# A layer norm, windowed attention and gated feed-forward kernel: from three phases with pooled order to one written-out pipeline over 512-token chunks

## The chip, the cores and the metric

The kernel runs on one core of a Trainium2 chip. The metric is device time in microseconds (us). Engine names: PE is TensorE's matmuls and PEld its weight loads, DVE is VectorE, ACT is ScalarE, POOL is GpSimd, and SP is SyncE, which here issues every DMA.

## What is computed

The input `x` has 2048 tokens of 512 features in bf16. Cut to what matters, the reference is:

```python
xn = _layernorm(x)                                   # no gain, no bias
# attention: H = 32 heads of Dh = 16, W = 8 taps, each 2 tokens apart, looking back
q, k, v = split(xn @ wqkv)                           # wqkv is 512 x 1536
logits = einsum("bhsd,bhswd->bhsw", q, k[s - 2*w]) * Dh ** -0.5   # masked where s - 2*w < 0
o = einsum("bhsw,bhswd->bhsd", softmax(logits), v[s - 2*w])
s = o @ wo                                           # wo is 512 x 512
# feed-forward: w_gate, w_up are 512 x 1792, w_down is 1792 x 512
y = (gelu_tanh(xn @ w_gate) * (xn @ w_up)) @ w_down
out = x + s * silu(y)
```

So each token has 8 logits in each of 32 heads, and each logit is a sum over 16 features.

## The kernel before

Weights stay in SBUF. The text of the kernel has phases over all 2048 tokens, and the tile framework's scheduler orders each engine's instructions by priority and readiness, so that pieces of the feed-forward land between the attention's.

1. **Layer norm** (L142 to L165): 16 tiles of 128 tokens. `bn_stats` and `bn_aggr` on DVE, the square root on ACT and a reciprocal on DVE for `rstd`, `xn_t` on DVE, four PE transposes into `tr_ps`, and a DVE copy into `xnT`.
2. **`qkv_phase`** (L181 to L204): for each of four 512-token chunks, 12 outputs of 128 features, each four matmuls of 512 columns. ACT copies `q_sb` and `k_sb` out of PSUM; `vst` goes to `vT_dram`.
3. **`attention_phase`** (L215 to L311): all four chunks lie side by side on the 128 partitions (chunk times head). For each of 8 taps and 4 feature groups DVE makes `prodk` (128 x 2048), and four matmuls with an indicator `ind1` of 128 columns, nearly all of them zero, sum the 16 features of each head into one `L_ps` of 128 rows. One Exp over 128 x 4096, a tree of DVE adds, one reciprocal of 128 x 512 and one multiplication make `attn`. For each of 16 features and 8 taps DVE makes `pv` (128 x 512), and PE adds the taps by multiplying with the identity into `oacc_ps`. The result goes through DRAM into `oT_fm`, and 64 matmuls with `wo_sb` give `s_sb`.
4. **`ffn_phase`** (L322 to L367): for each chunk 14 times four matmuls into `g_ps` and four into `u_ps`; ACT copies `u_bf`, squares `g_ps` and takes a tanh; DVE runs three `scalar_tensor_tensor`s, two of which read PSUM (L342, L347, L351). Then four tiles of 14 matmuls into `y_ps`, a tanh on ACT and one more DVE instruction for `g2`.
5. **Output** (L382 to L390): `x` is loaded a second time; DVE makes `bb` and `o_t`; SP stores.

The feed-forward and the attention have three PSUM banks each, and the transposes two.

Of the kernel before, what the change touches and what calls it, by code (L numbers as in the profile page):

```python
# [14 lines left out]
_DEBUG_MODE = 0
_FFN_FIRST = False
_PSUM_SPLIT = True
_H_ON_GPSIMD = False
# [3 lines left out]
def kernel(  # L22
# [10 lines left out]
):  # L33
    nc = tc.nc
    P = 128
    B, S, D = A_x.shape
    DF = B_w_gate.shape[1]
    H = 32
    DH = D // H
    W = 8  # L40
    DIL = 2
    PAD = 16
    assert (W - 1) * DIL <= PAD
    NT = S // P
# [39 lines left out]
    pstr = ctx.enter_context(tc.tile_pool(name="pstr", bufs=2, space=bass.MemoryType.PSUM))

    x_chunks = []
    for xc in range(NXC):
        xt = xpool.tile([P, XC, D], BF16, name="x_chunk")
# [12 lines left out]
    wu_sb = wpool.tile([P, NC, DF], BF16, name="wu_sb")
    nc.sync.dma_start(out=wu_sb[:], in_=B_w_up.rearrange("(k p) n -> p k n", p=P))
# [327 lines left out]
```

## Time and profile before

| what | us |
|---|---|
| median of 3 runs | 322.67 (322.48 to 322.85) |
| span of the profiled execution, first to last instruction | 319.8 |
| median of the runs less that span | 2.87 |
| DVE busy, share of the span | 245.1, 77% |
| ACT busy, share of the span | 165.8, 52% |

The profile gives the profiled execution as its span; what a run holds outside the span is the 2.87 us between the span and the median. Busy times are sums over the span, so they say nothing of which engine is waited for in a stage; the windows and the chain of waits do. A matmul's own duration (about 0.38 us for 512 columns) overlaps the next one, so PE's pace is read from a stretch and its count.

### The profile page before, as it was taken

How to read it: one execution, taken by the hardware profiler on the slowest of the kernel's cores; microseconds unless marked ns; L12 is line 12 of the kernel's file. 1: busy time of each engine (PE TensorE's matmuls, PEld its weight loads, DVE VectorE, ACT ScalarE, POOL GpSimd, SP SyncE). 2: the span in 40 equal slices, each digit the busy share in tenths (PEclk: the TensorE clock that was granted, in tenths of full speed). 3: DMA queues.
4: the chain of work that ended last, by engine and by line, in shares of the span. 5: the costliest groups of instructions: out<-in, count | busy, mean ns of one | idle time of the engine just before them, and what ended most of it. 6: DMA issues, size and time to landing. Idle time of an engine off the chain costs nothing.

```text
span 319.8 us, 3547 instructions
## 1 busy us (share of the span) xinstructions
PE 287.3 (90%) x1248; PEld 119.6 (37%) x1248; DVE 245.1 (77%) x460; ACT 165.8 (52%) x281; POOL 1.4 (0%) x10
## 2 busy tenths in 40 slices
PE   0698999999998576999999999999999999999993
PEld 0444444444433222444332343344443334443341
DVE  4867710159999699989999999944389995899954
ACT  1155986642201835622222488827558882588811
POOL 1000000000000000000000000000000000000000
PEclk9999999999999956999999999999999999999998
DMA  7997111110000093000000197102410001200012
GB/s 248 395 371 235 66 35 33 67 66 0 2 0 0 1 214 56 1 0 0 2 0 1 28 198 240 61 0 68 132 53 14 2 0 36 87 10 1 0 35 66
DMA packets 17762, 22.57 MB, mean 71 GB/s; under 512 B 1104, under 2 KB 15696, under 8 KB 17744
## 3 DMA queue, kind: packets, MB, share of 16 engines
q1 hardware_dynamic: 17744, 22.34, 23.3%
q8 instruction: 10, 0.16, 0.2%
q14 instruction: 8, 0.07, 0.1%
HBM read 16.04 MB, written 6.29 MB: 70 GB/s over the span
## 4 chain that ended last, share of the span: by engine, by line
PE 48%; DVE 30%; ACT 17%; issue 2%; DMA 1%; DVEq 0%; ACTq 0%
DVE pv L275 13%; PE qkv_ps L181 13%; PE y_ps L358 13%; PE L_ps L223 7%; ACT zt L345 7%; DVE zt L342 7%; ACT zt L341 7%; PE g_ps L322 5%; PE s_ps L304 4%; PE u_ps L331 4%; DVE prodk L215 3%; DVE stats L142 1%; ACT u_bf L339 1%; PE tr_ps L162 1%; DVE hT L351 1%
## 5 line engine op out<-in xcount | busy, mean ns | idle before, releaser
L322 PE MATMUL g_ps<-xnT,wg_sb 128*128 128x512 bf16 x224 | 61.5, 391 | 8.1 <-ACT u_bf L339 2.8
L331 PE MATMUL u_ps<-xnT,wu_sb 128*128 128x512 bf16 x224 | 60.7, 390 | 6.2 <-ACT u_bf L339 3.9
L215 DVE TENSOR_TENSOR prodk<-q_sb,k_sb 128x2048 bf16<-128x2048 bf16 x32 | 37.5, 1222 | 25.0 <-ACT k_sb L196 21.0
L358 PE MATMUL y_ps<-wd_sb,hT 128*128 128x512 bf16 x224 | 55.3, 379 | 0.6
L181 PE MATMUL qkv_ps<-xnT,wqkv_sb 128*128 128x512 bf16 x192 | 43.7, 387 | 0.0
L275 DVE TENSOR_TENSOR pv<-attn,v_arr 128x512 bf16<-128x512 bf16 x128 | 43.0, 416 | 0.0
L342 DVE SCALAR_TENSOR_TENSOR zt<-zt,g_ps 128x512 bf16<-128x512 bf16 x56 | 38.3, 684 | 5.5 <-ACT zt L341 0.7
L345 ACT ACTIVATE zt<-zt 128x512 bf16<-128x512 bf16 x56 | 35.2, 629 | 12.0 <-DVE zt L342 11.6
L281 PE MATMUL oacc_ps<-pv,ident 128*128 128x512 bf16 x128 | 41.2, 378 | 0.0
L351 DVE SCALAR_TENSOR_TENSOR hT<-zt,gu 128x512 bf16<-128x512 bf16 x56 | 38.4, 686 | 3.5 <-ACT zt L345 2.8
L339 ACT ACTIVATE u_bf<-u_ps 128x512 bf16<-128x512 f32 x56 | 33.2, 593 | 14.1 <-PE u_ps L331 13.6
L341 ACT ACTIVATE zt<-g_ps 128x512 bf16<-128x512 f32 x56 | 33.1, 596 | 13.9 <-PE g_ps L322 7.8
L347 DVE SCALAR_TENSOR_TENSOR gu<-g_ps,u_bf 128x512 bf16<-128x512 f32 x56 | 38.3, 684 | 0.2 <-ACT u_bf L339 0.2
L322 PEld LDWEIGHTS <-wg_sb 128*128 128x128 bf16 x224 | 22.1, 99 | 42.6 <-issue 22.8
L331 PEld LDWEIGHTS <-wu_sb 128*128 128x128 bf16 x224 | 22.2, 100 | 33.2 <-issue 9.3
L223 PE MATMUL L_ps<-prodk,ind 128*128 128x512 bf16 x128 | 32.6, 378 | 1.7 <-DVE prodk L215 0.9
L358 PEld LDWEIGHTS <-hT 128*128 128x128 bf16 x224 | 21.5, 97 | 29.0 <-issue 3.3
L181 PEld LDWEIGHTS <-wqkv_sb 128*128 128x128 bf16 x192 | 18.9, 100 | 21.5 <-issue 0.2
L288 ACT ACTIVATE o_arr<-oacc_ps 128x512 bf16<-128x512 f32 x16 | 9.6, 597 | 33.2 <-PE oacc_ps L281 33.2
L367 DVE SCALAR_TENSOR_TENSOR g<-th,y_ps 128x512 bf16<-128x512 bf16 x16 | 10.9, 686 | 20.3 <-ACT th L366 20.3
L366 ACT ACTIVATE th<-y_ps 128x512 bf16<-128x512 f32 x16 | 9.5, 597 | 31.0 <-PE y_ps L358 30.7
L281 PEld LDWEIGHTS <-ident 128*128 128x128 bf16 x128 | 11.7, 96 | 23.3 <-issue 9.5
(41 smaller groups left out, 153.8 us busy)
## 6 DMA issues: line engine op xcount, KB each, us to landing
x_chunk<-in_A_x_dram SPq DMA_DIRECT2D x4, 512.0 KB, 4.8
x_t<-in_A_x_dram SPq DMA_DIRECT2D x16, 128.0 KB, 2.3
vT_dram<-vst SPq DMA_DIRECT2D x16, 128.0 KB, 1.8
oT_dram<-o_arr SPq DMA_DIRECT2D x4, 512.0 KB, 7.8
oT_fm<-oT_dram SPq DMA_DIRECT2D x4, 512.0 KB, 5.2
out_dram<-o_t SPq DMA_DIRECT2D x16, 128.0 KB, 1.7
wg_sb<-in_B_w_gate_dram SPq DMA_DIRECT2D x1, 1792.0 KB, 14.7
wu_sb<-in_B_w_up_dram SPq DMA_DIRECT2D x1, 1792.0 KB, 9.2
```

The costliest lines, as they stand in the source:

```text
L181: nc.tensor.matmul(ps[:], lhsT=wqkv_sb[:, dk, fo * P : (fo + 1) * P], rhs=xnT[:, dk, jq * TQ : (jq + 1) * TQ], start=(dk == 0), stop=(dk = ...
L215: nc.vector.tensor_tensor(out=prodk[:], in0=q_sb[:, c, :], in1=k_sb[:, c, koff : koff + S], op=ALU.mult,)
L223: nc.tensor.matmul(L_ps[:], lhsT=ind1[:, IND1_OFF - o : IND1_OFF - o + P], rhs=prodk[:, jq * TQ : (jq + 1) * TQ], start=(c == 0 and jq == ...
L275: nc.vector.tensor_tensor(out=pv[:], in0=attn[:, w, :], in1=v_arr[:, d, voff : voff + TQ], op=ALU.mult,)
L281: nc.tensor.matmul(oacc_ps[:], lhsT=ident[:], rhs=pv[:], start=(w == 0), stop=(w == W - 1),)
L322: nc.tensor.matmul(g_ps[:], lhsT=wg_sb[:, dk, fc * P : (fc + 1) * P], rhs=xnT[:, dk, jq * TQ : (jq + 1) * TQ], start=(dk == 0), stop=(dk = ...
L331: nc.tensor.matmul(u_ps[:], lhsT=wu_sb[:, dk, fc * P : (fc + 1) * P], rhs=xnT[:, dk, jq * TQ : (jq + 1) * TQ], start=(dk == 0), stop=(dk = ...
L341: nc.scalar.activation(out=zt[:], in_=g_ps[:], func=AF.Square, scale=sqrt_c2)
L342: nc.vector.scalar_tensor_tensor(out=zt[:], in0=zt[:], scalar=c1, in1=g_ps[:], op0=ALU.add, op1=ALU.mult)
L345: nc.scalar.activation(out=zt[:], in_=zt[:], func=AF.Tanh)
L351: heng.scalar_tensor_tensor(out=hT[:, fc, :], in0=zt[:], scalar=1.0, in1=gu[:], op0=ALU.add, op1=ALU.mult)
L358: nc.tensor.matmul(y_ps[:], lhsT=hT[:, fc, tt * P : (tt + 1) * P], rhs=wd_sb[:, fc, :], start=(fc == 0), stop=(fc == NF - 1),)
```

## The change

The kernel's body is written anew. The scheduler is told to keep the order as written (`manual_schedule`), and the order is one pipeline over four chunks `j` of 512 tokens.

- **Layer norm** runs two chunks ahead, tile by tile. `rstd` is an addition and a power of -0.5 on POOL; the copy out of `tr` is on ACT. `x` stays in SBUF and is loaded once. The loads are cut smaller.
- **Logits**: the 128 partitions of `L_ps` now hold 4 taps times 32 heads of one chunk. DVE makes `pk` for one tap, all four feature groups at once (128 x 2048). The indicator `dsum[:, c, :]` has 32 columns; tap `wl` writes partitions `32*wl` to `32*wl + 31`, and four such matmuls, one for each tap, follow one another in `logits`.
- **Softmax**: Exp per half of the taps, straight from PSUM. `denominators` sums taps on PE (32-column `hsum`, 128 columns streamed), DVE takes one reciprocal of 128 x 128, `spread_reciprocals` lays it out by matmuls, and the division comes after the sum over taps, in the DVE instruction that makes `oT`.
- **Values**: `load_v` reads the chunk's `v` from DRAM four times, shifted by the tap. DVE makes `pv` for four features at once; `av_sum` adds over four taps on the partitions and two halves by 32-column matmuls, and its output has the layout that `wo` needs, so the attention's output no longer goes through DRAM.
- **Activations**: `Gelu_apprx_tanh` and `Silu` on ACT in place of the square, tanh and `scalar_tensor_tensor` chains; one DVE multiplication makes `h`.
- **PSUM**: five banks for projections, `y` and `s`; two for the attention; one for transposes.

The diff, cut to its core (removed lines are those of the kernel above; `project` is the same four-matmul loop as before, on `xnT[j]`):

```diff
+    ctx.enter_context(tc.manual_schedule())
...
+    prod = pool("prod", 8)
+    hp = pool("hp", 16)
...
+    sm = pool("sm", 3)
+    sm2 = pool("sm2", 2)
...
+    mm = pool("mm", 5, space=bass.MemoryType.PSUM)
+    att = pool("att", 2, space=bass.MemoryType.PSUM)
+    trp = pool("trp", 1, space=bass.MemoryType.PSUM)
...
+    for t in range(TPQ):
+        load_x(t)
+    for i in range(3):
+        load_w(wqkv_sb, A_wqkv, i * D, (i + 1) * D)
+    load_x(TPQ, TPQ)
+    for lo, hi in ((0, DF // 2), (DF // 2, DF)):
+        load_w(wg_sb, B_w_gate, lo, hi)
+        load_w(wu_sb, B_w_up, lo, hi)
     nc.sync.dma_start(out=wd_sb[:], in_=B_w_down.rearrange("(k p) n -> p k n", p=P))
+    load_x(2 * TPQ, TPQ)
+    load_x(3 * TPQ, TPQ)
+    for g in range(NC):
+        nc.sync.dma_start(
+            out=wo_sb[:, g, :],
+            in_=bass.AP(tensor=A_wo.tensor, offset=g * 4 * D, ap=[[D, 4], [DH * D, H], [1, D]]),
+        )
...
+    dsum = const.tile([P, NC, H], BF16, name="dsum")
+    nc.gpsimd.memset(dsum[:], 0.0)
+    for c in range(NC):
+        nc.gpsimd.memset(dsum[:, c, 8 * c : 8 * c + 8], 1.0)
+        band(dsum[:, c, 8 * c : 8 * c + 8], 0, 16, 16, 1, 8)
+    hsum = const.tile([P, H], BF16, name="hsum")
...
+    hsum = const.tile([P, H], BF16, name="hsum")
+    for j in range(WL):
+        nc.vector.tensor_copy(
+            out=hsum[H * j : H * (j + 1), :], in_=ident[H * j : H * (j + 1), H * j : H * (j + 1)]
+        )
...
+    def moments(t):
+        nc.vector.bn_stats(out=stats[:, t, :], in_=x_sb[:, t, :])
+        nc.vector.bn_aggr(out=mv[:, t, :], in_=stats[:, t, :])
+        nc.gpsimd.tensor_scalar(
+            out=rstd[:, t, :], in0=mv[:, t, 1:2], scalar1=EPS, scalar2=None, op0=ALU.add
+        )
+        nc.gpsimd.tensor_tensor(out=rstd[:, t, :], in0=rstd[:, t, :], in1=mhalf[:], op=ALU.pow)
+    def normalize(t):
+        xn = sm2.tile([P, D], BF16, name="xn")
+        nc.vector.tensor_scalar(
+            out=xn[:], in0=x_sb[:, t, :], scalar1=mv[:, t, 0:1], scalar2=rstd[:, t, :],
+            op0=ALU.subtract, op1=ALU.mult,
+        )
+        transpose(t, xn)
+    def transpose(t, xn):
+        tr = trp.tile([P, NC * P], BF16, name="tr")
+        for c in range(NC):
+            nc.tensor.transpose(tr[:, c * P : (c + 1) * P], xn[:, c * P : (c + 1) * P], ident[:])
+        j, i = divmod(t, TPQ)
+        if i == 0:
+            xnT[j] = xtp.tile([P, NC, TQ], BF16, name="xnT")
         nc.scalar.activation(
+            out=xnT[j][:, :, i * P : (i + 1) * P],
+            in_=tr[:].rearrange("p (c n) -> p c n", c=NC),
+            func=AF.Copy,
+        )
...
+    def qkv(j, fo):
+        which, c = divmod(fo, NC)
+        if fo == 0:
+            st[j]["q"] = qp.tile([P, NC, TQ], BF16, name="q_sb")
+        ps = mm.tile([P, TQ], F32, name="qkv_ps", tag="mm")
+        project(ps, wqkv_sb, fo * P, j)
+        if which == 0:
+            nc.scalar.activation(out=st[j]["q"][:, c, :], in_=ps[:], func=AF.Copy)
+        elif which == 1:
+            lo = PAD + j * TQ
+            nc.scalar.activation(out=k_sb[:, c, lo : lo + TQ], in_=ps[:], func=AF.Copy)
+        else:
+            vst = sm.tile([P, TQ], BF16, name="vst")
+            nc.scalar.activation(out=vst[:], in_=ps[:], func=AF.Copy)
+            lo = PAD + j * TQ
+            nc.sync.dma_start(out=vT[c * P : (c + 1) * P, lo : lo + TQ], in_=vst[:])
+    def load_v(j):
+        va = vap.tile([P, DH, VW], BF16, name="v_arr")
+        for wl in range(WL):
+            nc.sync.dma_start(
+                out=va[H * wl : H * (wl + 1), :, :],
+                in_=bass.AP(
+                    tensor=vT.tensor,
+                    offset=PAD + j * TQ - WL * DIL - DIL * wl,
+                    ap=[[SV * DH, H], [SV, DH], [1, VW]],
+                ),
+            )
+        st[j]["va"] = va
+    def qk_product(j, w):
+        pk = prod.tile([P, NC, TQ], BF16, name="pk", tag="prod")
+        off = PAD + j * TQ - w * DIL
         nc.vector.tensor_tensor(
+            out=pk[:], in0=st[j]["q"][:], in1=k_sb[:, :, off : off + TQ], op=ALU.mult
+        )
+        st[j]["pk"][w] = pk
+    def logits(j, wh):
+        L = att.tile([P, TQ], F32, name="L_ps", tag="att")
+        for c in range(NC):
+            for wl in range(WL):
                 nc.tensor.matmul(
+                    L[H * wl : H * (wl + 1), :],
+                    lhsT=dsum[:, c, :],
+                    rhs=st[j]["pk"][WL * wh + wl][:, c, :],
                     start=(c == 0),
                     stop=(c == NC - 1),
                 )
+        if wh == 0:
+            st[j]["E"] = ep.tile([P, WH, TQ], BF16, name="E")
+        E = st[j]["E"]
+        nc.scalar.activation(out=E[:, wh, :], in_=L[:], func=AF.Exp, scale=SCALE)
+        if j == 0:
+            for wl in range(WL):
+                w = WL * wh + wl
+                if w:
+                    nc.gpsimd.memset(E[H * wl : H * (wl + 1), wh, 0 : w * DIL], 0.0)
+    def denominators(j):
+        E = st[j]["E"]
+        den = att.tile([P, P], F32, name="den_ps", tag="att")
+        for wh in range(WH):
+            for q in range(4):
+                nc.tensor.matmul(
+                    den[H * q : H * (q + 1), :],
+                    lhsT=hsum[:],
+                    rhs=E[:, wh, q * P : (q + 1) * P],
+                    start=(wh == 0),
+                    stop=(wh == WH - 1),
                 )
+        rs = sm2.tile([P, P], BF16, name="rs")
+        with nc.allow_low_precision(reason="as the softmax of the reference"):
+            nc.vector.reciprocal(out=rs[:], in_=den[:])
+        st[j]["rs"] = rs
+    def spread_reciprocals(j):
+        sp = att.tile([P, TQ], F32, name="sp_ps", tag="att")
+        for q in range(4):
+            nc.tensor.matmul(
+                sp[:, q * P : (q + 1) * P], lhsT=spread[:, q, :], rhs=st[j]["rs"][:],
+                start=True, stop=True,
+            )
+        rb = op.tile([P, TQ], F32, name="rb")
+        nc.scalar.activation(out=rb[:], in_=sp[:], func=AF.Copy)
+        st[j]["rb"] = rb
+    def av_product(j, g, wh):
+        pv = prod.tile([P, 4, TQ], BF16, name="pv", tag="prod")
+        lo = WL * DIL * (1 - wh)
+        nc.vector.tensor_tensor(
+            out=pv[:],
+            in0=st[j]["E"][:, wh, :].unsqueeze(1).to_broadcast([P, 4, TQ]),
+            in1=st[j]["va"][:, 4 * g : 4 * g + 4, lo : lo + TQ],
+            op=ALU.mult,
+        )
+        st[j]["pv"][g, wh] = pv
+    def av_sum(j, g):
+        o = att.tile([P, TQ], F32, name="o_ps", tag="att")
+        for wh in range(WH):
+            for i in range(4):
+                nc.tensor.matmul(
+                    o[H * i : H * (i + 1), :],
+                    lhsT=hsum[:],
+                    rhs=st[j]["pv"][g, wh][:, i, :],
+                    start=(wh == 0),
+                    stop=(wh == WH - 1),
                 )
+        if g == 0:
+            st[j]["oT"] = op.tile([P, NC, TQ], BF16, name="oT")
+        nc.vector.tensor_tensor(
+            out=st[j]["oT"][:, g, :], in0=o[:], in1=st[j]["rb"][:], op=ALU.mult
+        )
+    def glu(j, fc):
+        g_ps = mm.tile([P, TQ], F32, name="g_ps", tag="mm")
+        project(g_ps, wg_sb, fc * P, j)
+        u_ps = mm.tile([P, TQ], F32, name="u_ps", tag="mm")
+        project(u_ps, wu_sb, fc * P, j)
+        ge = sm.tile([P, TQ], BF16, name="ge")
+        nc.scalar.activation(out=ge[:], in_=g_ps[:], func=AF.Gelu_apprx_tanh)
+        u = sm.tile([P, TQ], BF16, name="u")
+        nc.scalar.activation(out=u[:], in_=u_ps[:], func=AF.Copy)
+        h = hp.tile([P, TQ], BF16, name="h")
+        nc.vector.tensor_tensor(out=h[:], in0=ge[:], in1=u[:], op=ALU.mult)
+        st[j][fc] = h
+    def down(j, tt):
+        y = mm.tile([P, D], F32, name="y_ps", tag="mm")
+        for fc in range(NF):
+            nc.tensor.matmul(
+                y[:],
+                lhsT=st[j][fc][:, tt * P : (tt + 1) * P],
+                rhs=wd_sb[:, fc, :],
+                start=(fc == 0),
+                stop=(fc == NF - 1),
+            )
+        sl = sm2.tile([P, D], BF16, name="sl")
+        nc.scalar.activation(out=sl[:], in_=y[:], func=AF.Silu)
+        s = mm.tile([P, D], F32, name="s_ps", tag="mm")
+        for g in range(NC):
+            nc.tensor.matmul(
+                s[:],
+                lhsT=st[j]["oT"][:, g, tt * P : (tt + 1) * P],
+                rhs=wo_sb[:, g, :],
+                start=(g == 0),
+                stop=(g == NC - 1),
+            )
+        t = j * TPQ + tt
+        m = sm2.tile([P, D], BF16, name="m")
+        nc.vector.tensor_tensor(out=m[:], in0=s[:], in1=sl[:], op=ALU.mult)
+        o_t = sm2.tile([P, D], BF16, name="o_t")
+        nc.vector.tensor_tensor(out=o_t[:], in0=m[:], in1=x_sb[:, t, :], op=ALU.add)
+        nc.sync.dma_start(out=out2d[t * P : (t + 1) * P, :], in_=o_t[:])
+    for t in range(TPQ):
+        moments(t)
+        if t:
+            normalize(t - 1)
+    normalize(TPQ - 1)
+    for t in range(TPQ, 2 * TPQ):
+        moments(t)
+    for fo in range(3 * NC):
+        qkv(0, fo)
+        if fo in (2, 4, 6, 8):
+            normalize(TPQ + fo // 2 - 1)
+    load_v(0)
+    for j in range(NJ):
+        for fc in range(NF):
+            if j == 0:
+                if fc < W:
+                    qk_product(j, fc)
+                if fc == 5:
+                    logits(j, 0)
+                if fc == 9:
+                    logits(j, 1)
+                if fc == 11:
+                    denominators(j)
+                if fc == 13:
+                    spread_reciprocals(j)
+                    av_product(j, 0, 0)
+                    av_product(j, 0, 1)
             else:
+                if fc == 0:
+                    logits(j, 1)
+                if fc == 1:
+                    denominators(j)
+                if fc == 3:
+                    spread_reciprocals(j)
+                if fc in (5, 7, 9, 11):
+                    av_sum(j, (fc - 5) // 2)
+                if 2 <= fc < 10:
+                    av_product(j, (fc - 2) // 2, fc % 2)
+            glu(j, fc)
+        if j == 0:
+            for i in range(12):
+                qkv(1, i)
+                if i in (1, 4, 7, 10):
+                    g = i // 3
+                    av_sum(0, g)
+                    if g < 3:
+                        av_product(0, g + 1, 0)
+                        av_product(0, g + 1, 1)
+        elif j + 1 < NJ:
+            for i in range(12):
+                qkv(j + 1, i)
+                if i % 3 == 0 and j + 2 < NJ:
+                    moments((j + 2) * TPQ + i // 3)
+                if i % 3 == 2 and j + 2 < NJ:
+                    normalize((j + 2) * TPQ + i // 3)
+        if j + 1 < NJ:
+            load_v(j + 1)
+        for tt in range(TPQ):
+            if j + 1 < NJ:
+                if tt == 2:
+                    logits(j + 1, 0)
+                qk_product(j + 1, 2 * tt)
+                qk_product(j + 1, 2 * tt + 1)
+            if j == 0:
+                moments(2 * TPQ + tt)
+            down(j, tt)
+            if j == 0:
+                normalize(2 * TPQ + tt)
```

## Rows read from the trace of the kernel before

**Rows 1.** The page, part 1: busy us, share of the span, instructions of each engine.

```profile
PE 287.3 (90%) x1248; PEld 119.6 (37%) x1248; DVE 245.1 (77%) x460; ACT 165.8 (52%) x281; POOL 1.4 (0%) x10
```

**Rows 2.** The page, part 4: chain that ended last, shares by engine.

```profile
PE 48%; DVE 30%; ACT 17%; issue 2%; DMA 1%; DVEq 0%; ACTq 0%
```

**Rows 3.** Windows: stretch, length, busy (count) of PE, PEld, DVE, ACT, POOL; clock; DMA.

```profile
68.00:104.00 36.00, 34.42 (x146) 13.79 (x145) 35.09 (x31) 7.17 (x12) 0.00 (x0) 1.00 0.03 9
104.00:116.00 12.00, 7.53 (x26) 2.60 (x25) 9.55 (x22) 8.31 (x10) 0.00 (x0) 0.84 0.36 76
116.00:131.00 15.00, 11.42 (x36) 4.01 (x35) 14.68 (x19) 7.87 (x15) 0.00 (x0) 0.68 0.47 84
137.30:180.40 43.10, 43.10 (x164) 14.68 (x163) 43.10 (x130) 10.15 (x17) 0.00 (x0) 1.00 0.00 1
181.00:208.00 27.00, 25.80 (x112) 10.87 (x112) 24.89 (x40) 23.16 (x42) 0.00 (x0) 1.00 0.60 156
```

**Rows 4.** The chain in order of time: start us, us, engine and line, count.

```profile
38.51 29.45 PE qkv_ps L181 x136
...
302.23 12.30 PE y_ps L358 x56
...
316.63 0.42 DVE o_t L389
```

**Rows 5.** Groups of instructions: shapes, count, busy us, mean ns, idle before.

```profile
L215 DVE TENSOR_TENSOR prodk<-q_sb,k_sb 128x2048 bf16<-128x2048 bf16 x32 | 37.5, 1222 | 25.0 <-ACT k_sb L196 21.0 <-PE L_ps L223 4.0
L342 DVE SCALAR_TENSOR_TENSOR zt<-zt,g_ps 128x512 bf16<-128x512 bf16 x56 | 38.3, 684 | 5.5 <-ACT zt L341 0.7
L281 PE MATMUL oacc_ps<-pv,ident 128*128 128x512 bf16 x128 | 41.2, 378 | 0.0
L281 PEld LDWEIGHTS <-ident 128*128 128x128 bf16 x128 | 11.7, 96 | 23.3 <-issue 9.5 <-DVE pv L275 5.8
L142 DVE BATCH_NORM_STATS2 stats<-x_chunk 128x6 f32<-128x512 bf16 x16 | 10.5, 669 | 5.1 <-DMA x_chunk<-in_A_x_dram 5.1
L389 DVE TENSOR_TENSOR o_t<-bb,x_t 128x512 bf16<-128x512 bf16 x16 | 6.7, 423 | 5.1 <-DMA x_t<-in_A_x_dram 4.8
L259 DVE RECIPROCAL rs<-ssum 128x512 f32<-128x512 f32 x1 | 3.3, 3344 | 0.0
L262 DVE TENSOR_TENSOR attn<-attn,rs 128x4096 bf16<-128x4096 bf16 x1 | 2.3, 2280 | 0.0
```

**Rows 6.** ACT's timeline around a change of its function table.

```profile
27.94 0.60 ACT L339 ACTIVATE u_bf<-u_ps 128x512 bf16<-128x512 f32 x1 [0.63 <-PE u_ps L331]
28.56 1.28 ACT L345 ACT_TABLE_LOAD   x1
29.85 0.63 ACT L345 ACTIVATE zt<-zt 128x512 bf16<-128x512 bf16 x1
```

**Rows 7.** PE's timeline at its start: start us, us, line, count.

```profile
10.22 2.36 PE L162 MATMUL tr_ps<-ident,xn_t 128*128 128x128 bf16 x16 [10.22 <-DVE xn_t L152]
...
13.17 1.06 PE L181 MATMUL qkv_ps<-xnT,wqkv_sb 128*128 128x512 bf16 x2
...
16.55 0.39 PE L162 MATMUL tr_ps<-ident,xn_t 128*128 128x128 bf16 x4
16.78 3.40 PE L181 MATMUL qkv_ps<-xnT,wqkv_sb 128*128 128x512 bf16 x15
```

**Rows 8.** The page, part 6: DMA issues, count, KB each, median us to landing.

```profile
x_t<-in_A_x_dram SPq DMA_DIRECT2D x16, 128.0 KB, 2.3
vT_dram<-vst SPq DMA_DIRECT2D x16, 128.0 KB, 1.8
...
v_arr<-vT_dram SPq DMA_DIRECT2D x3, 528.0 KB, 9.0
```

**Rows 9.** SP's timeline: the first issue, and one that took long.

```profile
0.80 1.00 SPq L89 DMA_DIRECT2D x_chunk<-in_A_x_dram  x2
...
16.98 7.81 SPq L382 DMA_DIRECT2D x_t<-in_A_x_dram  x2
```

More of the change, by code (lines that the diff above doesn't have):

```diff
@@ L5 @@
 import concourse.tile as tile
[L6 removed]
+from concourse import mybir
 from concourse._compat import with_exitstack
@@ L11 @@
 AF = mybir.ActivationFunctionType
-AX = mybir.AxisListType
 BF16 = mybir.dt.bfloat16
 F32 = mybir.dt.float32
[L15 to L18, printed above, removed]
+P = 128
+H = 32
+DH = 16
+W = 8
+DIL = 2
+WL = 4
+WH = 2
+PAD = 16
+TQ = 512
+VW = TQ + WL * DIL
+EPS = 1e-5
+SCALE = DH ** -0.5
 @with_exitstack
@@ L84, with pool @@
[L84 to L88, printed above, removed]
+    NT, NC, NF, NJ = S // P, D // P, DF // P, S // TQ
+    TPQ = TQ // P
+    SV = PAD + S
+    x2d, out2d = A_x[0], out[0]
+    ctx.enter_context(tc.manual_schedule())
+    def pool(name, bufs, **kw):
+        return ctx.enter_context(tc.tile_pool(name=name, bufs=bufs, **kw))
+    const = pool("const", 1)
@@ L131 @@
-    eps_sb = cpool.tile([P, 1], F32, name="eps_sb")
-    nc.vector.memset(eps_sb[:], EPS)
-    xnT = xnpool.tile([P, NC, S], BF16, name="xnT")
-    stats = cpool.tile([P, NT, nc.vector.BN_STATS_DIM], F32, name="stats")
-    mv = cpool.tile([P, NT, nc.vector.BN_AGGR_DIM], F32, name="mv")
-    rstd = cpool.tile([P, NT, 1], F32, name="rstd")
-    for xc in range(NXC):
-        xt = x_chunks[xc]
-        for i in range(XC):
-            t = xc * XC + i
-            nc.vector.bn_stats(out=stats[:, t, :], in_=xt[:, i, :])
-            nc.vector.bn_aggr(out=mv[:, t, :], in_=stats[:, t, :])
-        ts = slice(xc * XC, (xc + 1) * XC)
+            out=x_sb[:, t : t + n, :],
@@ new lines, with band @@
+    nc.sync.dma_start(out=vT.rearrange("(k p) n -> p k n", p=P)[:, :, 0:PAD], in_=zpad[:])
+    def band(dst, lo_base, hi_base, step, mult, n):
+        nc.gpsimd.affine_select(
+            out=dst, in_=dst, pattern=[[-step, n]], compare_op=ALU.is_ge, fill=0.0,
+            base=lo_base, channel_multiplier=mult,
+        )
+        nc.gpsimd.affine_select(
+            out=dst, in_=dst, pattern=[[step, n]], compare_op=ALU.is_gt, fill=0.0,
+            base=hi_base, channel_multiplier=-mult,
+        )
@@ new lines @@
+    nc.vector.memset(spread[:], 0.0)
+    for q in range(4):
+        for j in range(4):
+            nc.vector.tensor_copy(
+                out=spread[H * q : H * (q + 1), q, H * j : H * (j + 1)],
+                in_=ident[H * q : H * (q + 1), H * q : H * (q + 1)],
+            )
+    xnT = {}
+    k_sb = big.tile([P, NC, PAD + S], BF16, name="k_sb")
+    nc.vector.memset(k_sb[:, :, 0:PAD], 0.0)
+    stats = const.tile([P, NT, nc.vector.BN_STATS_DIM], F32, name="stats")
+    mv = const.tile([P, NT, nc.vector.BN_AGGR_DIM], F32, name="mv")
@@ new lines @@
+    mhalf = const.tile([P, 1], F32, name="mhalf")
+    nc.gpsimd.memset(mhalf[:], -0.5)
+    rstd = const.tile([P, NT, 1], F32, name="rstd")
+    def moments(t):
[5 more added lines that the diff above has]
+        nc.gpsimd.tensor_tensor(out=rstd[:, t, :], in0=rstd[:, t, :], in1=mhalf[:], op=ALU.pow)
```

344 lines of the change are left out of this document (34 added, 310 removed).

## The prediction, made before the changed kernel was run

> **What bounds the kernel now.** I read the page first, then the chain of waits, then windows by stage. The page shows PE busy for 90% of the span and DVE for 77% [rows 1]. A busy PE is not a PE at its pace, so I take the pace from two stretches in which it waits for nothing: 136 matmuls in 29.45 us, 0.2165 each, and 56 of `y` in 12.30, 0.2196 each [rows 4]. The kernel has 1184 matmuls of 512 columns (192 qkv, 128 + 128 in the attention, 64 for `s`, 3 times 224 in the feed-forward); at 0.2165 they are 256.3 us of the 319.8. The other 63 us are what PE spends waiting, besides transposes.
>
> The chain says for whom: DVE has 30% of it and ACT 17% [rows 2]. The windows say where [rows 3]. From 104 to 131 us PE issues 62 matmuls, 13.4 us of work in 27, at a granted clock of 0.84 and 0.68, while DVE and ACT work through the softmax. From 137.3 to 180.4, where DVE is busy for all of it with `pv`, 164 matmuls (35.5 us) fill 43.1. From 68 to 104, 146 (31.6) fill 36, with DVE busy for 35.1. In the feed-forward's window from 181 to 208, 112 matmuls (24.2) take 27.0, with DVE at 24.9: its three long instructions per output pace it. So PE's own work is 80% of the time and DVE's nearly all the rest. Before the first qkv matmul 13.17 us pass [rows 7].
>
> **The change, step by step.** I build the new span from PE's list, because every other engine gets less than PE has.
>
> *DVE.* Now 32 products of 128 x 2048 for the logits (1.22 each), 32 for the values, 56 `h` and 16 `o_t` at 0.42, 16 `m` and 16 `oT` reading PSUM at 0.68, stats and `xn` of 16 tiles at 0.67 + 0.17 + 0.42, four reciprocals of 128 columns at 3.34/4 [rows 5]. The values' product multiplies a broadcast tile; the nearest row is `attn<-attn,rs`, also a broadcast, 2.28 for 4096 columns, so 1.2 for 2048. The sum is 39 + 39 + 30 + 22 + 20 + 3 = 153 us, against 245. In glu steps 2 to 9 DVE has 1.2 + 0.42 + about 0.34 = 2.0 us per step, about PE's own 1.73 + 0.3, and nothing on PE waits for `h` there. DVE leaves the path but in places named below.
>
> *ACT.* 204 activations of about 0.60 are 122 us. Exp, Gelu and Silu each follow one another in the written order, and I count 21 changes of function (5 in glu 0, then Silu, Exp, Silu in each of three down stages, Exp and Gelu at each later glu, a last Silu). A change costs, from the end of the copy at 28.54 to the next start at 29.85, 1.31 us [rows 6]: 27 us, 150 in all of some 260. What hides them is PSUM: the worst place is glu 5 of chunk 0, where load, Exp, load and Gelu end 3.3 us after `L_ps` is done, while PE can fill five banks, 4.3 us, before it needs that one back. Cost nothing; without that cover it would be the 3.3 us each time. The Trainium skill (ScalarE: Activation LUTs, What ACT_TABLE_LOAD costs) speaks against interleaving functions of different table sets: it adds a drain of about 1.38 us, 2.66 per switch. The trace has the 1283 ns load and no such drain beside it. By the page ACT would carry 56 us of switches, the wait at glu 5 and 9 would outlast the banks by 1.7 us each, and the sum would be 3.4 us higher.
>
> *PE, full-width work.* 704 matmuls (qkv, gate, up, `s`) at 0.2165 are 152.4; 224 of `y` at 0.2196 are 49.2. Together **201.6**.
>
> *PE, 32-column work.* `logits` and `av_sum` replace 256 full-width matmuls (55.4 us) by 256 with 32 weight columns, in 64 groups of four. The four of a group use a quarter of the columns each and write four different strips of 32 partitions. No row shows such a matmul. Bounds: all four in one slot, 0.2165 a group, 13.9 us; or one slot each, 55.4 us. I take one slot and, since the four bring their own weights, one weight load of 0.096 [rows 5]: 0.31 a group, **20.0**. I stand near the lower end because the rows' slot is the time to stream 512 columns and not the time to use all weight columns, and nothing in the diff ties one strip to another. The Trainium skill (TensorE: Matmul & The Clock Gate, Part 3: Packing small matmuls) measured 2.38 times for three strips side by side; at that rate, an estimate, four matmuls would take 0.36 and the sum be 3 us higher.
>
> *PE, changes of width.* The 28 blocks with 32 columns (8 `logits`, 16 `av_sum`, 4 `denominators`) may each cost nothing or, both ways, what a matmul lasts beyond its slot: 0.378 - 0.2165 = 0.16 [rows 5]; 0 to 9.2 us. I take one way, **4.5**.
>
> *PE, small work.* 48 matmuls of 128 columns for the denominators and their spreading, and the transposes of 12 later tiles: four take 0.39 [rows 7], so 24 times 0.39, **9.4**.
>
> *Start.* SP's first issue is at 0.80 [rows 9], 128 KB land in 2.3 [rows 8], so the first tile is there at 3.1, where before a 512 KB load and eight tiles' stats came first. Four tiles of stats (0.67) and `xn` (0.42) in turn on DVE end at 7.5; POOL's two small instructions for the last `rstd`, which no row shows and which may cost 0.2 or several us, I put at 0.5; transposes and ACT's copy 1.1 to 1.5: first qkv at **9.6**. PE was slow at first before as well: two qkv took 1.06 at 13.17, and 15 took 3.40 only from 16.78, 6.6 us after its first transpose [rows 7]. The same delay from a first transpose at 6.5 leaves 3.5 us of qkv at half pace, **1.7**.
>
> *Waits that the order makes.* (a) `vst` has three buffers and its stores stand on SP behind all loads, the same 9.4 MB as before, where SP sat 7.81 us in two issues and came free at 24.8 [rows 9]. The fourth `vst`, due near 24, waits for the first store to land, near 27; ACT stands, with the Gelus behind it, and PE's four free banks (3.5 us) cover most: 0 to 3, I take 1.5. (b) In qkv(1), `av_sum` g+1 comes 2.6 us after g, but DVE needs `oT` and two products, 0.7 + 2.4: 0.6 three times, 1.8. (c) In down(0), PE's transposes stand in order behind `m`, `o_t` and `xn` of the same step: 0.68 + 0.42 + 0.42 after `s` and an estimated 0.13 of hand-overs, 1.65 each, four times, 6.6. `y` of the next tile is queued behind them. Together **9.9**. `load_v` later is hidden: three transfers of 528 KB took 9.0 us to land [rows 8], and a down stage of 16 us and two glu steps lie before its first use. The attention's trip through DRAM and the second load of `x` were hidden too and give nothing.
>
> *End.* After the last `s`: `m` 0.68, `o_t` 0.42, and from the end of `o_t` at 317.05 to 319.8 [rows 4] 2.75: **3.9**.
>
> The sum is 201.6 + 20.0 + 4.5 + 9.4 + 9.6 + 1.7 + 9.9 + 3.9 = 260.6 us of span. The runs' median is 2.87 above the profiled span, so 263.5.
>
> **The rivals.**
>
> *The strips take turns.* If each 32-column matmul takes a slot of its own, its term is 55.4 instead of 20.0: 298.9. For it speaks that every row here shows matmuls one after another at 0.2165; against it, that none of these had columns left over. This is the claim that the change's layout rests on not doing what it says.
>
> *The broadcast product is slow.* If `av_product` ran at the pace of the PSUM reads (0.684 per 512, 2.7 for 2048), DVE would need 3.5 us per glu step from 2 to 9 against PE's 2.05: 8 x 1.4 in three chunks and some 9 in qkv(1), 43 more: 306. The row of 2.28 for a 4096-column broadcast speaks against it.
>
> *Slower: moving to another strip empties PE.* If each 32-column matmul had to end before the next began, it would cost 0.378 and a weight load of 0.096, 0.474, 256 times 121 us: 101 more, 365. The point from which this decides is 0.31 per matmul (59 us above the 20.0). Against it speaks that here matmuls with new weights each time start 0.2165 apart though each lasts 0.378 [rows 4, 5], so new weights alone do not empty PE.
>
> *Fewer waits.* With the groups at one slot, no cost for changes of width and half the waits, 248.
>
> **How the numbers follow.** I give my forecast 0.72, the strips in turn 0.14, the slow product 0.05, the emptied PE 0.03, still fewer waits 0.06. The forecast's own range is 249 to 282: below, the lower bounds of strips (6), widths (4.5) and half the waits; above, widths both ways (4.5), waits doubled (10) and POOL slow at the start (4). With the strips in turn at 298.9 the range for all is 249 to 300, which leaves out some 0.2. A measurement here tells 0.2%, 0.65 us, from no change. All but the emptied PE end below that: faster 0.96, same 0.01, slower 0.03.
>
> **What would show it.** In the new profile: starts of `L_ps` matmuls in fours close together, and `logits` with 16 of them in about 1.3 us (3.5 would be strips in turn); DVE near 150 us busy and ACT near 150; about 21 table loads with no PE wait behind them; first qkv near 10 us; glu stages near 29 us, where the feed-forward window had 27.0 for less work; waits of PE for `xn` near 1.65 in down(0) and nowhere later. The prediction fails if the strips do not overlap, or if PE shows waits of over a microsecond at places other than (a) to (c).

## The result, and the profile after

The changed kernel takes 271.25 us (median of 4 runs, 269.82 to 272.64) against 322.58 beside it: a ratio of 0.843 (95% interval 0.839 to 0.847). The forecast was 263.5. The profiled execution took 271.04 us with a span of 269.3; the forecast of the span was 260.6. One of the four runs of e4 below (270.84) and one of the ten of e10 (325.10), each over 1.5% above the fastest run of the same kernel, were slow ones and are left out of the medians and ratios.

From the page: busy times as in [rows 1], and the chain by engine as in [rows 2].

```profile
PE 235.2 (87%) x1296; PEld 100.3 (37%) x1296; DVE 148.3 (55%) x242; ACT 146.8 (55%) x226; POOL 16.2 (6%) x60
...
PE 71%; SPq 11%; DMA 9%; DVE 6%; issue 1%; ACT 0%; POOL 0%; DVEq 0%; ACTq 0%
```

DVE went from 245.1 us to 148.3 (forecast 153), and ACT has 146.8 (forecast 150). DVE's part of the chain fell from 30% to 6%. New in the chain are SP's issues and DMAs, 20% together, where before DMA had 1%. The list of waits says who stands (engine and line, waited for, us in total, times, longest):

```profile
PE tr L179 <- DVE xn L170: 14.2, 6, 6.8
...
ACT vst L214 <- DMA vT<-vst: 12.0, 1, 12.0
...
PE g_ps L191 <- ACT vst L214: 9.0, 1, 9.0
...
DVE o_t L356 <- DMA out_dram<-o_t: 6.0, 2, 3.9
...
PE L_ps L244 <- DVE pk L235: 4.0, 4, 2.1
```

The longest wait of `tr`, 6.8, is the start of the kernel. The others each have their place in the chain in order of time (start us, us, what, count):

```profile
30.25 6.02 DMA vT<-vst
36.38 0.61 ACT vst L214
37.03 1.87 PE g_ps L191 x4
38.94 1.86 PE u_ps L191 x4
40.80 1.44 PE g_ps L191 x4
42.25 0.86 PE u_ps L191 x4
...
44.84 0.98 PE L_ps L244 x16
45.81 0.97 PE g_ps L191 x4
46.78 0.86 PE u_ps L191 x4
...
111.95 0.55 PE o_ps L305 x8
...
147.54 10.37 DMA out_dram<-o_t
158.43 0.63 DVE pk L235
...
208.71 8.60 DMA out_dram<-o_t
217.44 2.36 DVE pk L235 x2
219.85 1.87 PE L_ps L244 x13
221.72 1.50 PE g_ps L191 x4
...
265.33 0.70 DVE m L354
```

Three things are to be seen. Sixteen 32-column matmuls take 0.98 us and eight take 0.55, where a slot each would be 3.46 and 1.73. Near 30 us the chain leaves PE for a store of `vst`, and PE's first matmuls after it are slow, 1.87 for four and not 0.86. And twice, at 147 and 209 us, it runs through the landing of an output store of 128 KB, which took 10.37 and 8.60 us, to a late `pk` and a late `L_ps`.

PE in windows around the wait for `vst` (stretch, length, busy and count, granted clock, DMA share, GB/s), and then all engines in glu(2), with columns as in [rows 3]:

```profile
28.00:30.00 2.00, 0.03 (x1) 1.00 0.44 145
30.00:32.00 2.00, 0.00 (x0) 0.90 0.38 101
32.00:34.00 2.00, 0.00 (x0) 0.50 0.70 237
...
37.00:39.00 2.00, 1.93 (x5) 0.50 0.19 66
...
42.30:45.00 2.70, 2.70 (x19) 1.00 1.11 191
```

```profile
160.80:189.30 28.50, 28.47 (x170) 11.81 (x170) 18.88 (x28) 18.38 (x30) 0.00 (x0) 1.00 0.02 5
```

PE issues nothing from 28 us on; the granted clock falls to 0.50, the lower level of 1.2 GHz, while it stands, stays there for the first matmuls after 37 us, and is back at 1.00 (2.4 GHz) by 42.3. In glu(2), 112 full-width matmuls, most of an `L_ps`, four `o_ps`, the denominators and their spreading take 28.5 us with PE never waiting, against 27.0 for the 112 alone in [rows 3].

### The profile page after: what moved, and what is told of

Read it like the earlier page. It is cut to its first block, busy times and chain, and to the rows that moved or that the text cites. A ratio compares the mean times of both kernels' runs of the same rounds, so it can differ in the third digit from the quotient of the medians.

```text
span 269.3 us, 3429 instructions
## 1 busy us (share of the span) xinstructions
PE 235.2 (87%) x1296; PEld 100.3 (37%) x1296; DVE 148.3 (55%) x242; ACT 146.8 (55%) x226; POOL 16.2 (6%) x60
## 4 chain that ended last, share of the span: by engine, by line
PE 71%; SPq 11%; DMA 9%; DVE 6%; issue 1%; ACT 0%; POOL 0%; DVEq 0%; ACTq 0%
PE g_ps L191 19%; PE u_ps L191 18%; PE y_ps L334 12%; PE qkv_ps L191 11%; DMA out_dram<-o_t 7%; SPq L83 4%; PE s_ps L345 4%; PE o_ps L305 3%; PE L_ps L244 3%; SPq L89 3%; SPq L105 2%; DMA vT<-vst 2%; DVE m L354 2%; DVE pk L235 2%; DVE o_t L356 1%
## 5 line engine op out<-in xcount | busy, mean ns | idle before, releaser
L328 DVE TENSOR_TENSOR h<-ge,u 128x512 bf16<-128x512 bf16 x56 | 23.7, 423 | 59.7 <-ACT u L326 59.6
L334 PE MATMUL y_ps<-wd_sb,h 128*128 128x512 bf16 x224 | 51.0, 379 | 0.0
L235 DVE TENSOR_TENSOR pk<-q_sb,k_sb 128x2048 bf16<-128x2048 bf16 x32 | 38.0, 1219 | 9.4 <-ACT k_sb L211 9.4
L324 ACT ACTIVATE ge<-g_ps 128x512 bf16<-128x512 f32 x56 | 33.6, 599 | 16.7 <-PE g_ps L191 16.6
L326 ACT ACTIVATE u<-u_ps 128x512 bf16<-128x512 f32 x56 | 33.5, 598 | 14.0 <-PE u_ps L191 14.0
L293 DVE TENSOR_TENSOR pv<-E,v_arr 128x2048 bf16<-128x2048 bf16 x32 | 38.6, 1217 | 0.0
L334 PEld LDWEIGHTS <-h 128*128 128x128 bf16 x224 | 21.5, 98 | 26.3 <-issue 1.3
L354 DVE TENSOR_TENSOR m<-s_ps,sl 128x512 bf16<-128x512 f32 x16 | 11.1, 691 | 29.7 <-PE s_ps L345 29.7
L345 PE MATMUL s_ps<-wo_sb,oT 128*128 128x512 bf16 x64 | 16.4, 379 | 0.0
L244 PE MATMUL L_ps<-pk,dsum 128*32 128x512 bf16 x128 | 10.9, 406 | 4.0 <-DVE pk L235 4.0
## 6 DMA issues: line engine op xcount, KB each, us to landing
v_arr<-vT SPq DMA_DIRECT2D x16, 520.0 KB, 10.2
```

Of the source, the lines that this page charges most:

```text
L235: nc.vector.tensor_tensor(out=pk[:], in0=st[j]["q"][:], in1=k_sb[:, :, off : off + TQ], op=ALU.mult)
L244: nc.tensor.matmul(L[H * wl : H * (wl + 1), :], lhsT=dsum[:, c, :], rhs=st[j]["pk"][WL * wh + wl][:, c, :], start=(c == 0), stop=(c == NC ...
L293: nc.vector.tensor_tensor(out=pv[:], in0=st[j]["E"][:, wh, :].unsqueeze(1).to_broadcast([P, 4, TQ]), in1=st[j]["va"][:, 4 * g : 4 * g + 4, ...
L324: nc.scalar.activation(out=ge[:], in_=g_ps[:], func=AF.Gelu_apprx_tanh)
L326: nc.scalar.activation(out=u[:], in_=u_ps[:], func=AF.Copy)
L328: nc.vector.tensor_tensor(out=h[:], in0=ge[:], in1=u[:], op=ALU.mult)
```

## The experiments

Each run was made against the kernel before on the same chip; the times are medians, and the ratios have 95% intervals. Not all runs were on one chip; the kernel before took 321.71 to 322.67 beside them, so differences between two rows of under 1 us say little.

| run | us | ratio to before |
|---|---|---|
| the change | 271.25 | 0.843 (0.839 to 0.847) |
| e1, four `vst` buffers | 261.09 | 0.812 (0.807 to 0.817) |
| e2, loads behind the stores | 262.37 | 0.817 (0.812 to 0.822) |
| e3, no `o_t` buffer | 263.63 | 0.821 (0.817 to 0.825) |
| e4, transposes one tile later | 266.65 | 0.828 (0.823 to 0.834) |
| e5, strips in another order | 270.74 | 0.841 (0.837 to 0.845) |
| e6, one function table | 272.46 | 0.846 (0.843 to 0.849) |
| e7, before with Gelu and Silu | 300.59 | 0.932 (0.930 to 0.935) |
| e8, e1 + e3 + e4 | 246.04 | 0.763 (0.761 to 0.766) |
| e9, order left to the scheduler | 254.33 | 0.790 (0.788 to 0.792) |
| e10, change with the old activations | 321.96 | 0.999 (0.997 to 1.002) |
| e11, one strip for all logits | 286.42 | 0.889 (0.887 to 0.892) |
| e12, e8 and the start | 244.24 | 0.759 (0.757 to 0.761) |

### The stores behind the loads (e1, e2)

SP's timeline of the changed kernel (start us, us, issue), and then the first `vst` in ACT's:

```profile
12.71 9.11 SPq L83 DMA_DIRECT2D x_sb<-in_A_x_dram  x2
21.86 6.80 SPq L105 DMA_DIRECT2D wo_sb<-in_A_wo_dram  x4
28.79 1.36 SPq L115 DMA_DIRECT2D vT<-zpad  x1
30.25 7.07 SPq L216 DMA_DIRECT2D vT<-vst  x4
```

```profile
21.80 0.60 ACT L214 ACTIVATE vst<-qkv_ps 128x512 bf16<-128x512 f32 x1 [0.27 <-PE qkv_ps L191]
```

The first `vst` was ready at 22.4 us (21.80 + 0.60); SP came to its store at 30.25.

```diff
+    vstp = pool("vstp", 4)
-            vst = sm.tile([P, TQ], BF16, name="vst")
+            vst = vstp.tile([P, TQ], BF16, name="vst")
```

> The changed kernel with four buffers for vst instead of three. Buffer theory: ACT's 12.0 us wait for the first store, and PE's 9.0 us behind it, are gone, and so are the four slow groups of matmuls after it (1.87, 1.86, 1.44 us where 0.86 is the pace, 2.6 us together): 271 - 11.6, about 260. The stores land no earlier, so load_v lands near 50 us and must not be waited for before glu step 13, which comes near 52. Rival: the wait only moves to the late v_arr and less than 5 us come back, 266 to 271.

It gave 261.09, 10.2 less (11.6 expected). ACT's timeline in e1, at the fourth `vst` and the function change behind it:

```profile
25.82 0.60 ACT L215 ACTIVATE vst<-qkv_ps 128x512 bf16<-128x512 f32 x1 [0.27 <-PE qkv_ps L192]
26.44 1.28 ACT L325 ACT_TABLE_LOAD   x1
27.73 0.60 ACT L325 ACTIVATE ge<-g_ps 128x512 bf16<-128x512 f32 x1
```

The wait is gone, and no other of its size took its place: of PE's waits that e1 could have lengthened, the one of `L_ps` for `pk` went from 4.0 us to 4.5. e2 leaves the three buffers and moves the loads of `x` for the last two chunks and of `wo` behind `load_v(0)`:

```diff
-    load_x(2 * TPQ, TPQ)
-    load_x(3 * TPQ, TPQ)
-    for g in range(NC): ...   # the four wo loads
     load_v(0)
+    load_x(2 * TPQ, TPQ)
...
```

> The changed kernel with three buffers for vst as it is, but the loads of x for chunks 2 and 3 and of wo (1.5 MB) issued on SP after load_v(0). Queue theory: the first store is issued near 22 us in place of 30 and lands near 26, the fourth vst waits 1 to 2 us and PE not at all: about 260, as with a fourth buffer. Rival: the bytes do not matter but the 512 small pieces of the zero store do, which still stands ahead of the stores; then ACT's wait shrinks by less than half and the time stays above 266.

It gave 262.37. ACT's fourth `vst` in e2:

```profile
28.18 0.60 ACT L207 ACTIVATE vst<-qkv_ps 128x512 bf16<-128x512 f32 x1 [3.64 <-DMA vT<-vst]
```

ACT now waits 3.64 us and not 12.0. That is more than the 1 to 2 expected, as the first store, issued at 22.61, took 5.6 us to land; PE's free banks cover most of it, and PE stands for 0.6. So it is the place in SP's queue; the zero store, which still stands ahead of the stores in e2, is not the main part. Either cure is enough.

### The output stores behind load_v (e3)

```diff
-        o_t = sm2.tile([P, D], BF16, name="o_t")
-        nc.vector.tensor_tensor(out=o_t[:], in0=m[:], in1=x_sb[:, t, :], op=ALU.add)
+        nc.vector.tensor_tensor(out=x_sb[:, t, :], in0=m[:], in1=x_sb[:, t, :], op=ALU.add)
```

> The changed kernel with the sum of the output written over x's own tile instead of into one of two o_t buffers, so that the third output of a chunk waits for no store. Queue theory: DVE's two waits for stores queued behind load_v (6.0 us) are gone, pk is in time, and L_ps at the end of down(1) and down(2) takes 1.0 us: 1.9 + 4.5 + 0.5 less, about 264.5. Rival: pk is late because DVE itself has too much in the down stage; then under 2 us come back, 269 to 271.

It gave 263.63, 7.6 less (6.9 expected): the queue theory. Neither PE's wait for `pk` nor DVE's for an output store is in its list of waits. SP's rows of the changed kernel show the place of the stores at the end of down(1):

```profile
144.69 2.67 SPq L222 DMA_DIRECT2D v_arr<-vT  x4
...
147.54 14.66 SPq L357 DMA_DIRECT2D out_dram<-o_t  x4
```

The store of the first output stands behind four loads of 520 KB and lands 10.37 us after its issue, the two buffers are used up, and DVE stops in front of `o_t` with the next chunk's `pk` behind it.

### The transposes of down(0) (e4)

```diff
-            if j == 0:
-                normalize(2 * TPQ + tt)      # xn on DVE, then four transposes on PE
+            if j == 0:                       # the transposes go out in the next tile, ahead of s
+                late.append((2 * TPQ + tt, normalize(2 * TPQ + tt)))
```

> The changed kernel with the four transposes of a tile in down(0) issued on PE after the next tile's y instead of right behind s; DVE's order is as it was. Order theory: PE's four waits of 1.64 us for xn are gone and down(0) goes from 24.8 to 18 to 20 us: 264.5 to 266. Rival: DVE, which needs 4.7 us a tile there (two pk, moments, m, sum, xn), sets the pace at 4.7 against PE's 4.3; then only 1.2 us a tile come back, about 266.5 to 267.

It gave 266.65, 4.6 less. Its runs (265.74 to 268.36) reach from the order theory's range past the rival's, so the time does not decide, and the trace has to. PE's waits for `xn` of 1.64 are gone, with one of 0.81 in their place; the wait list and the chain of e4 show what came instead:

```profile
DVE o_t L360 <- DMA out_dram<-o_t: 10.2, 3, 4.1
...
PE L_ps L244 <- DVE pk L235: 6.7, 5, 2.3
```

```profile
81.94 9.96 DMA out_dram<-o_t
...
92.00 0.42 DVE o_t L360
```

The faster down(0) ran into the output stores behind `load_v(1)`, a third place of e3's wait, which PE's slowness had covered. With e3 in place (e8) the four tiles of down(0) and both logits blocks take 18.3 us, from 66.60 to 84.87, with PE never waiting, so DVE does not set the pace either.

### What makes the 32-column matmuls cheap (e5, e11)

```diff
-        for c in range(NC):
-            for wl in range(WL):
+        for wl in range(WL):
+            for c in range(NC):
                 nc.tensor.matmul(L[H * wl : H * (wl + 1), :], ...)
```

(and the same exchange in `av_sum`.)

> The changed kernel with the same 32-column matmuls in another order: all that write one strip of 32 partitions follow one another (in L_ps four, in o_ps two), then the next strip. Overlap theory: matmuls on different strips run side by side, those on one strip do not; L_ps then takes 13 slots, 2.8 us instead of 0.98, and o_ps 5 slots, 1.08 instead of 0.55: 14.6 + 8.5 more, about 294; without overlap where the strip changes, up to 310. Rival: a matmul with 32 columns is simply short, whatever stands next to it: 271.

It gave 270.74: no difference, as the rival had it. The trace's single starts tell why, and that the rival's reason does not follow. Starts in us of one `L_ps` block in the changed kernel and in e5, and of the block of e5 at the end of down(1), where the `pk` of the last two taps are late:

```
change: 101.602 .606 .609 .612 | 101.829 .832 .836 .839 | 102.045 .048 .052 .055 | 102.261 .264 .267 .271
e5:     101.789 .803 .816 .829 | 102.015 .029 .042 .055 | 102.231 .244 .258 .271 | 102.447 .460 .474 .487
e5, late pk: 159.212 .225 | 159.438 .451 | 159.654 .667 | 159.869 .883
             160.726 | 160.941 | 161.156 | 161.371
             161.862 | 162.077 | 162.292 | 162.507
```

In the first two, four start within 10 ns (the changed kernel) or 40 (e5), and the next four 0.216 to 0.227 us after. In e5 four neighbours in the program write the same strip, so these fours cannot be program neighbours: each strip goes on with its own. My expectation assumed that a matmul waiting for its strip holds up those behind it; it does not: the first of the fourth strip started with nine issued before it still waiting. The late block shows the strips apart: while the `pk` of two taps are there, their two strips start in pairs 13 ns apart; the third and then the fourth strip, whose `pk` come later, run alone, and each of their four matmuls takes a slot of 0.216. To tell "short" from "side by side", e11 lets all 16 write one strip:

```diff
+        nc.tensor.matmul(L[:], lhsT=ident[:], rhs=st[j]["pk"][WL * wh][:, 0, :], start=True, stop=True)
-                    L[H * wl : H * (wl + 1), :],
+                    L[0:H, :],
```

> The changed kernel with all 16 matmuls of each logits block writing the same 32 partitions, after one full-width matmul that fills the bank; the logits are not what is to be computed. Strip theory: what lets four run at once is that they use different strips, whatever the order they are issued in; on one strip the 16 take a slot each, 3.46 us and 0.22 for the fill in place of 0.98, 8 times 2.7: 290 to 294. Rival: a matmul with 32 weight columns is short by itself: 8 x 0.22 more, 273.

Every block of e11's chain reads as this one does:

```profile
110.54 3.56 PE L_ps L247 x16
```

Sixteen starts 0.216 apart (0.227 the first time): 3.56 us against 0.98. So a 32-column matmul costs a full slot, and the four strips are what makes four of them cost one. The time rose by 15.2 us and not by 19 to 23: in the changed kernel late `pk` cost `L_ps` 6.9 us, and that wait is not in e11's list; 8 times 2.8 less 6.9 is 15.5. I take it that the longer blocks give DVE the time to catch up.

The Trainium skill (TensorE: Matmul & The Clock Gate, Part 3: Packing small matmuls) describes strips that run concurrently and start about 4 ns apart. The trace agrees, with 3 to 4 ns in the written order. The Trainium skill's 2.38 times is for three strips. Here, on four strips, a group of four goes out in the 0.216 us that a single matmul takes in e11, so the stream runs four times as fast, and block against block it is 3.6 times (3.56/0.98).

### Function tables (e6)

```diff
-func=AF.Gelu_apprx_tanh
+func=AF.Tanh                      # also in place of AF.Silu
```

> The changed kernel with Tanh in the place of Gelu and of Silu, so that every activation's function lies in one table and one table load is left of 22; the gate and the output's gate are not computed. Cover theory: the 21 loads, 27 us of ACT, are hidden behind PSUM's banks: 270 to 271.5. Rival: ACT's switches are on the path at glu 5 and 9 and at each later glu 0, 3.3 us each: 255 to 262.

The page of e6:

```profile
PE 233.7 (86%) x1271; PEld 100.4 (37%) x1296; DVE 148.8 (55%) x242; ACT 121.4 (45%) x205; POOL 16.3 (6%) x60
```

ACT fell to 121.4 us, and the time is 272.46, 1.2 more than the change with runs that overlap: the 21 loads are covered. They stay so where PE's other waits are cured: in e8 PE waits for ACT only at the start, for `xnT`. In e1's rows above a switch costs 1.31 us from the end of `vst` at 26.42 to the start of `ge` at 27.73, the load's 1.28 and nothing beside it. The Trainium skill's (ScalarE: Activation LUTs, What ACT_TABLE_LOAD costs) 1.38 us of drain does not show here either.

### Which part of the change gives the time (e7, e9, e10)

e7 is the kernel before with the new activations:

```diff
-                # square, tanh and three scalar_tensor_tensor
+                nc.scalar.activation(out=ge[:], in_=g_ps[:], func=AF.Gelu_apprx_tanh)
+                nc.vector.tensor_tensor(out=hT[:, fc, :], in0=ge[:], in1=u_bf[:], op=ALU.mult)
...
+                nc.scalar.activation(out=g2[:, t, :], in_=y_ps[:], func=AF.Silu)
```

> The kernel before with one part of the change alone: Gelu and Silu on ACT, one DVE multiplication for hT, and nothing else. Pipeline theory: DVE loses 91 + 11 us of work, the feed-forward's windows run at PE's pace (3 a chunk less), but the attention is still paced by pv and prodk in its two windows and by the softmax: 295 to 310. Rival: the activations alone are what the change gives: 270 to 280.

e10 is the changed kernel with the old feed-forward chain (the reverse of that edit in `glu`, and 14 buffers for `h`).

> The changed kernel with the feed-forward's old activation chain (square, tanh and three scalar_tensor_tensor) in place of Gelu and one multiplication, and 14 buffers for h to make room. DVE theory: DVE gets 56 x (3 x 0.684 - 0.423) = 91 us more, and in glu steps with a product it has 3.6 us against PE's 2.1 or less: 310 to 325, so the pipeline without the activations gives little. Rival: DVE's idle 45% takes it: under 285.

e9 takes out `ctx.enter_context(tc.manual_schedule())` and nothing else.

> The changed kernel without the written order: the framework's scheduler may reorder each engine's instructions by priority and readiness, as it did before. Order theory: the written order is part of the gain, and letting go of it brings new waits or a late attention: 275 to 295. Rival: the scheduler moves other matmuls into the places where PE stands for vst, xn and pk, and ends at 250 to 268.

The activations alone give 22 us (300.59), the pipeline alone nothing (321.96), both inside the first range given for them; together they give 51. In e10 DVE has 231.5 us of work again, and PE stands for its products:

```profile
PE 247.1 (77%) x1296; PEld 103.2 (32%) x1296; DVE 231.5 (72%) x354; ACT 160.7 (50%) x274; POOL 16.2 (5%) x60
...
PE o_ps L305 <- DVE pv L293: 29.4, 16, 2.6
```

So here PE's saved matmuls are worth time only once DVE has room. e9 gave 254.33, as the rival had it: the order as written costs 17 us against the scheduler's own. In e9 PE waits for 0.2 us after its first qkv, which comes only at 15.59 us; on ACT, for one, the scheduler puts six activations of the feed-forward ahead of the fourth `vst`. So the written order is not where the gain of the change comes from. With its waits cured (e8 below) the written order is 8.3 us faster than e9; the scheduler's order with the same cures was not run.

### Together (e8, e12)

> The changed kernel with three edits together: four buffers for vst, the output's sum in x's tile, transposes of down(0) after the next y. If the three waits are separate: 271 - 11.6 - 6.9 - 5 = 247 to 249. If they share a cause, 252 to 258.

It gave 246.04, 25.2 less; e1, e3 and e4 alone sum to 22.4. The rest fits what e4 alone lost to the stores: there `L_ps` waited 6.7 us for `pk`, in the change 4.0. e12 adds the start:

```diff
     normalize(TPQ - 1)                # dsum, hsum and spread are built here, not ahead of the layer norm
+        if t in (1, 3):
+            tr = att.tile([P, NC * P], BF16, name="tr1", tag="att")
...
+                if fc == 12 and j + 2 < NJ:
+                    moments((j + 2) * TPQ)   # and the later moments one step earlier
```

> The three fixes together, and three more at places where PE still waits: the constants hsum, spread and dsum are built after the first chunk's layer norm and not ahead of it (0.9 us, as x lands near 3.5 and DVE came free at 4.4), the first chunk's transposes alternate between two PSUM banks (0.6 to 1.5), and the moments of chunk 3 are taken one step earlier (1.0): 246 - 2.5, 242.5 to 244.5. Rival: the start is bound by the loads of wqkv, and nothing comes back: 245.5 to 246.5.

It gave 244.24, inside its range, and 1.8 less than e8 with intervals that just touch. PE's first qkv stands at 10.02 us, against 11.86 in e8 and in the change:

```profile
10.02 4.42 PE L174 MATMUL qkv_ps<-xnT,wqkv_sb 128*128 128x512 bf16 x10 [0.68 <-ACT xnT L166]
```

e12 is the fastest kernel of the study, 24% under the one before, and its PE is busy for 95% of the span.

## Why the prediction was right, and where not

| term | forecast | in the trace after |
|---|---|---|
| first qkv at | 9.6 | 11.86 |
| slow matmuls at first | 1.7 | 1.3 (12 in 4.06, of which 0.38 is the last one's) |
| full-width matmuls | 201.6 | 200.3 (928 at 0.2158, qkv(3): 48 in 10.36) |
| strips and changes of width | 20.0 + 4.5 | 19.3 (8 x 0.98, 16 x 0.55, 24 x 0.11 after them) |
| small work | 9.4 | 4.4 (12 transposes of 0.22, denominators 0.23, spreading 0.22) |
| (a) stores of `vst` | 1.5 | 9.0 and 2.6 of slow matmuls |
| (b) `av_sum` in qkv(1) | 1.8 | 0.6 |
| (c) `xn` in down(0) | 6.6 | 6.6 |
| waits not named | 0 | 6.9 for `L_ps` at the ends of down(1) and down(2), 0.8 for `xn` in qkv(2) |
| end | 3.9 | 4.1 |

The right column sums to 267.8 of the span's 269.3. The terms that came out shorter than forecast take off 13.1 us, those that came out longer add 20.3. That the time lies only 7.8 us above the forecast is so in part luck: errors of both signs cancel.

The forecast also added 2.87 us for what a run holds outside the span. A run holds less: 271.04 - 269.3 = 1.7 here, and 1.8 in the runs of the kernel before whose span is on record (322.01 against 320.2). The rest of the 2.87 is that the profiled execution of before was some 1 us shorter than the median.

The direction and its reason held. DVE left the path by the amounts forecast: `pv` with its broadcast tile took 1.217 us for 2048 columns, `h` 0.423. The strips ran together, as the likeliest case had it, and at the lower bound: no weight load shows in a group of four, which takes 0.216 and not 0.31. Changes of width cost 0.11 into a block and 0.11 out. Two terms were too long because a row's length holds the last matmul's own 0.38 us: in [rows 7] the four transposes take 0.39, but the next matmul starts 0.23 after them, and that is what the small work costs in the trace after; and `y` runs at 3.02/14 = 0.216, not 0.2196. The order's wait (c) came as worked out:

```profile
82.42 0.40 PE L179 MATMUL tr<-ident,xn 128*128 128x128 bf16 x4 [1.64 <-DVE xn L170]
```

The mis-sized step is (a): "waits for the first store to land, near 27". It landed at 36.3. I took SP to be free at 24.8, as before. But about the same bytes now come in more issues and smaller pieces, of which `wo`'s four alone hold SP from 21.86 to 28.66; no run tells whether the number of issues or the size of the pieces does it. The store then took 6.02 us from issue to landing, where 1.7 is the least, which I read as its bytes standing behind what is still queued. And I counted only the wait and not the clock after it.

The step that failed is "`load_v` later is hidden". `load_v` itself is; the output stores that SP issues behind it are not, since DVE has two `o_t` buffers and the next `pk` queued behind the third. e3 shows it. This term stood at nothing and came to 6.9 us: 4.0 of waits for `pk`, the longest 2.1, and the rest matmuls that ran alone between the waits or at a low granted clock after them (0.50 from 220 to 222 us). By the prediction's own last sentence, a wait of over a microsecond outside (a) to (c) is a sign of failing, and here is one; the time came out inside the range all the same.

At the start, two things were missing from the sum, besides POOL's two instructions for `rstd`, which took 0.22 + 0.57 and not 0.5. DVE built 20 small constants (0.16 to 0.18 us each) ahead of the first `stats`, which so began at 4.37; and with one `tr` bank a tile's transposes wait for ACT's copy of the last:

```profile
8.05 0.59 PE L179 MATMUL tr<-ident,xn 128*128 128x128 bf16 x4 [0.69 <-ACT xnT L183]
...
9.32 0.58 PE L179 MATMUL tr<-ident,xn 128*128 128x128 bf16 x4 [0.69 <-ACT xnT L183]
```

The other rivals fell: no product was slow, no strip emptied PE.

## What to carry to other kernels

Where a sum needs only 32 output rows, give four such sums four strips of the output's partitions; it pays only if the engine that feeds them has room, so count that engine first. In a fixed order, look at what stands behind each DMA in its queue: a store whose buffer someone needs back must not be issued behind bulk loads. A wait that is cured may uncover the next one, so cures are tried together as well as alone, and against the order the scheduler would choose.

## What the hardware showed that was not expected

Matmuls on one strip do not hold up later ones on other strips, even when four in a row go to one strip (e5). And a wait of 9.0 us cost PE 2.6 us more: four matmuls then took 1.87, 1.86 and 1.44 us where 0.86 is the pace, with the granted clock at 0.50 in the window from 37 to 39 us.
